# Cutting HBM into blocks of 8, 60 and 60 rows per partition in a streaming x + gamma*y kernel, with the small block loaded first and stored in the middle

## The chip, the core and the metric

The kernel runs on one core of a Trainium2 chip. Time is device time in microseconds (us), as the median over several executions. Spans and packet durations come from one profiled execution of each kernel.

## The reference

```python
# x, y: [1024, 16, 512] bfloat16, gamma: [512] bfloat16
def reference(x, y, gamma):
    return x + gamma * y
```

Flattened, x and y are 16384 rows of 512 elements, 1 KB each. Each of the 128 SBUF partitions gets 128 rows. Reading x and y and writing the result moves 3 x 16.78 = 50.33 MB, and there is little arithmetic.

## The kernel before

Partition p holds rows 128p to 128p + 127, so the same row of neighbouring partitions lies 128 KiB apart in HBM. The loads go out on SyncE's queue in the order of the list `SP`, the stores on ScalarE's in the order of `ACT`. VectorE works in place on y, in four pieces; `m` is the multiply by gamma, `a` the addition of x.

```python
PIECES = [53, 11, 53, 11]
SP = [('y', 0, 4), ('y', 4, 64), ('x', 0, 64, 0), ('y', 64, 128), ('x', 64, 117, 0), ('x', 117, 128, 64)]
ACT = [('g',), ('s', 0, 64), ('s', 64, 128)]
RELEASE = ('x', 64, 117, 0)
DVE = [('m', 0), ('m', 1), ('a', 0), ('a', 1), ('m', 2), ('m', 3), ('a', 2), ('a', 3)]
...
xv = xf.rearrange("(p n) d -> p n d", p=P)      # the same for y and out
...
# a load of x waits until the adds that read its buffer slots are done;
# the first store waits until RELEASE has landed, and every store for its adds
```

An entry `('x', 64, 117, 0)` loads rows 64 to 117 of every partition into slot 0 and up of x's buffer. That buffer has fewer slots than there are rows, so this load has to wait for the first add. The first two loads are issued ahead of everything else. The first store is released by the landing of `RELEASE`, so that stores do not share the DMA engines with the loads that VectorE needs.

Of the kernel before, what the change touches and what calls it, by code (L numbers as in the profile page):

```python
# [3 lines left out]


PIECES = [53, 11, 53, 11]



SP = [('y', 0, 4), ('y', 4, 64), ('x', 0, 64, 0), ('y', 64, 128), ('x', 64, 117, 0), ('x', 117, 128, 64)]  # L10
ACT = [('g',), ('s', 0, 64), ('s', 64, 128)]

EARLY = (2, 0)


RELEASE = ('x', 64, 117, 0)

DVE = [('m', 0), ('m', 1), ('a', 0), ('a', 1), ('m', 2), ('m', 3), ('a', 2), ('a', 3)]
MULT, ADD = mybir.AluOpType.mult, mybir.AluOpType.add


def _take(sem, n, eng):


    return eng.wait_ge(sem, n).then_inc(sem, -n)  # L25


def kernel(
# [10 lines left out]
    P = nc.NUM_PARTITIONS  # L39
# [3 lines left out]
    xf = x.flatten_outer_dims()  # L43
    yf = y.flatten_outer_dims()
    of = out.flatten_outer_dims()
    N, D = xf.shape
    rows = N // P
    n = len(PIECES)
    assert sum(PIECES) == rows
    starts = [sum(PIECES[:c]) for c in range(n + 1)]  # L50
    dt = xf.dtype
    xv = xf.rearrange("(p n) d -> p n d", p=P)
    yv = yf.rearrange("(p n) d -> p n d", p=P)
    ov = of.rearrange("(p n) d -> p n d", p=P)

    gamma_row = nc.alloc_sbuf_tensor("gamma_row", [1, D], dt).ap()
    ones_row = nc.alloc_sbuf_tensor("ones_row", [1, P], dt).ap()
# [1 line left out]
    y_sb = nc.alloc_sbuf_tensor("y_sb", [P, rows, D], dt).ap()  # L59
    x_loads = [w for w in SP + ACT if w[0] == "x"]  # L60
    y_loads = [w for w in SP + ACT if w[0] == "y"]
    stores = [w for w in SP + ACT if w[0] == "s"]
    for loads in (x_loads, y_loads, stores):
# [7 lines left out]
    s_load = {w: sem("s_" + "_".join(map(str, w[:2]))) for w in x_loads + y_loads}  # L71
    s_add, s_go, s_rel, s_end, s_out = sem("s_add"), sem("s_go"), sem("s_rel"), sem("s_end"), sem("s_out")
    added = [a for kind, *a in DVE if kind == "a"]
    order = {a[0]: k for k, a in enumerate(added)}

    def meets(a, b, c, d):
        return a < d and c < b

    def pieces_of(a, b):
        return [c for c in range(n) if meets(starts[c], starts[c + 1], a, b)]  # L80

    def x_at(row):
        return next(w[3] + row - w[1] for w in x_loads if w[1] <= row < w[2])

    def frees(w):

        c = set()
        for v in x_loads[: x_loads.index(w)]:
            lo, hi = max(v[3], w[3]), min(v[3] + v[2] - v[1], w[3] + w[2] - w[1])
            if lo < hi:  # L90
                c |= set(pieces_of(v[1] + lo - v[3], v[1] + hi - v[3]))
        return sorted(c)
# [3 lines left out]
    def ring(eng, what, n_early):  # L96

        known, went = 0, False
        for k, w in enumerate(what):
            kind = w[0]  # L100
            need = frees(w) if kind == "x" else pieces_of(w[1], w[2]) + list(w[3:]) if kind == "s" else []
            need = max((order[c] + 1 for c in need), default=0)
            if kind == "s" and not went:
                _take(s_go, 1, eng)
                went = True
            if need > known:
                eng.wait_ge(s_add, need)
                known = need
            if kind == "g":
                i = eng.dma_start(out=gamma_row, in_=gamma.unsqueeze(0)).then_inc(s_gamma, 16)  # L110
            elif kind == "x":
                to = x_sb[:, w[3] : w[3] + w[2] - w[1], :]
                i = eng.dma_start(out=to, in_=xv[:, w[1] : w[2], :]).then_inc(s_load[w], 16)
            elif kind == "y":
                r = slice(w[1], w[2])
                i = eng.dma_start(out=y_sb[:, r, :], in_=yv[:, r, :]).then_inc(s_load[w], 16)
            else:
                r = slice(w[1], w[2])
                i = eng.dma_start(out=ov[:, r, :], in_=y_sb[:, r, :]).then_inc(s_out, 16)
            if k < n_early:  # L120
                early.append(i.ins)

    ring(nc.sync, SP, EARLY[0])
    ring(nc.scalar, ACT, EARLY[1])


# [7 lines left out]

    _take(s_load[RELEASE], 16, nc.tensor)
    nc.tensor.sem_inc(s_go, 1)
# [4 lines left out]
    def need(loads, c):  # L141
        for w in loads:
            if w not in landed and meets(starts[c], starts[c + 1], w[1], w[2]):
                if w == RELEASE:
                    _take(s_rel, 1, nc.vector)
                else:
                    _take(s_load[w], 16, nc.vector)
                landed.add(w)

    for kind, *args in DVE:  # L150
        c = args[0]
        yt = y_sb[:, starts[c] : starts[c + 1], :]
        if kind == "m":
            need(y_loads, c)
            g = gamma_sb[:, None, :].to_broadcast([P, PIECES[c], D])
            nc.vector.tensor_tensor(out=yt, in0=yt, in1=g, op=MULT).then_inc(s_dve, 1)  # L156
            open_mults += 1
        else:
# [4 lines left out]
            at = x_at(starts[c])  # L163
            xt = x_sb[:, at : at + PIECES[c], :]
            nc.vector.tensor_tensor(out=yt, in0=xt, in1=yt, op=ADD).then_inc(s_add, 1)  # L165
# [44 lines left out]
```

## Time and profile before

| | before |
|---|---|
| median time | 120.06 us |
| profiled span | 118.7 us |
| VectorE busy | 70.0 us (59%) |
| packets in the 16 DMA engines | 98.6% of the span |
| bytes, mean rate | 50.33 MB, 424 GB/s |
| 64 KB packet | 2418 ns, loads and stores alike |

Some figures here and below come from the trace's record of each DMA packet (start, duration, size, queue), summed over the packets and divided by 16 engines. "Idle" is the time in which fewer than 16 packets are in flight, weighted by how many are missing. "Extra" is what packets take above 0.03677 ns per byte + 8.4 ns.

### The profile page before, as it was taken

How to read it: one execution, taken by the hardware profiler on the slowest of the kernel's cores; microseconds unless marked ns; L12 is line 12 of the kernel's file. 1: busy time of each engine (PE TensorE's matmuls, PEld its weight loads, DVE VectorE, ACT ScalarE, POOL GpSimd, SP SyncE). 2: the span in 40 equal slices, each digit the busy share in tenths (PEclk: the TensorE clock that was granted, in tenths of full speed). 3: DMA queues.
4: the chain of work that ended last, by engine and by line, in shares of the span. 5: the costliest groups of instructions: out<-in, count | busy, mean ns of one | idle time of the engine just before them, and what ended most of it. 6: DMA issues, size and time to landing. Idle time of an engine off the chain costs nothing. (4 is left out here: it accounts for less than half of the span.)

```text
span 118.7 us, 80 instructions
## 1 busy us (share of the span) xinstructions
PE 0.6 (0%) x1; PEld 0.1 (0%) x1; DVE 70.0 (59%) x10; POOL 0.2 (0%) x4
## 2 busy tenths in 40 slices
PE   0001000000000000000000000000000000000000
PEld 0000000000000000000000000000000000000000
DVE  0002000599999299999759999999999910000000
POOL 0000000000000000000000000000000000000000
DMA  8977977998899888998896969498899889988891
GB/s 268 571 332 331 663 331 331 596 464 353 353 486 574 353 353 353 640 420 353 353 585 293 585 293 585 205 634 353 353 596 464 353 353 420 640 353 353 353 663 44
DMA packets 1154, 50.33 MB, mean 424 GB/s; under 512 B 129, under 2 KB 130, under 8 KB 258
## 3 DMA queue, kind: packets, MB, share of 16 engines
q1 hardware_dynamic: 864, 33.55, 66.0%
q10 hardware_dynamic: 290, 16.78, 32.6%
HBM read 33.56 MB, written 16.78 MB: 424 GB/s over the span
## 5 line engine op out<-in xcount | busy, mean ns | idle before, releaser
L156 DVE TENSOR_TENSOR y_sb<-y_sb,gamma_sb 128x27136 bf16<-128x27136 bf16 (+1 forms) x4 | 34.6, 8688 | 12.3 <-DVEq L25 12.3
L165 DVE TENSOR_TENSOR y_sb<-x_sb,y_sb 128x27136 bf16<-128x27136 bf16 (+1 forms) x4 | 34.6, 8689 | 2.3 <-DVEq L25 2.2
L132 DVE CAST gamma_sb<-gamma_ps 128x512 bf16<-128x512 f32 x1 | 0.7, 692 | 8.8 <-DVEq L25 8.8
L127 DVE MEMSET ones_row<- 1x128 bf16 x1 | 0.2, 165 | 2.0 <-PEq L41 2.0
L130 PE MATMUL gamma_ps<-gamma_row,ones_row 1*128 1x512 bf16 x1 | 0.6, 577 | 10.2 <-PEq L25 10.2
L130 PEld LDWEIGHTS gamma_ps<-gamma_row,ones_row 1*128 1x128 bf16 x1 | 0.1, 99 | 10.2 <-issue 10.2
L194 POOL MEMSET const-bfloat16-1.0<- 128x1 bf16 x1 | 0.1, 101 | 0.0
L194 POOL MEMSET const-uint8-127<- 128x1 uint8 x1 | 0.1, 101 | 0.0
L194 POOL MEMSET const-float32-0.0<- 128x1 f32 x1 | 0.1, 98 | 0.2 <-issue 0.2
L194 POOL MEMSET const-float32-1.0<- 128x1 f32 x1 | 0.1, 98 | 0.0
## 6 DMA issues: line engine op xcount, KB each, us to landing
y_sb<-in_y_dram SPq DMA_DIRECT2D x1, 7680.0 KB, 21.4
x_sb<-in_x_dram SPq DMA_DIRECT2D x1, 6784.0 KB, 20.8
x_sb<-in_x_dram SPq DMA_DIRECT2D x1, 1408.0 KB, 23.8
y_sb<-in_y_dram SPq DMA_DIRECT2D x1, 512.0 KB, 3.8
out_dram<-y_sb ACTq DMA_DIRECT2D x2, 22.8
x_sb<-in_x_dram SPq DMA_DIRECT2D x1, 39.3
gamma_row<-in_gamma_dram ACTq DMA_DIRECT2D x1, 1.0 KB
y_sb<-in_y_dram SPq DMA_DIRECT2D x1, 58.3
```

The costliest lines, as they stand in the source:

```text
L127: nc.vector.memset(ones_row, 1.0).then_inc(s_ones, 1)
L130: nc.tensor.matmul(gamma_ps, ones_row, gamma_row, start=True, stop=True).then_inc(s_ps, 1)
L132: nc.vector.tensor_copy(out=gamma_sb, in_=gamma_ps).then_inc(s_dve, 1)
L156: nc.vector.tensor_tensor(out=yt, in0=yt, in1=g, op=MULT).then_inc(s_dve, 1)
L165: nc.vector.tensor_tensor(out=yt, in0=xt, in1=yt, op=ADD).then_inc(s_add, 1)
L194: nc = _bacc.Bacc("TRN2", target_bir_lowering=False, num_devices=1)
```

## The change

The intent is to make each block that is loaded or stored contiguous in HBM, to begin with a small contiguous block of y, and to put that block's store between the two large stores.

```diff
+BLOCKS = [8, 60, 60]
-PIECES = [53, 11, 53, 11]
+PIECES = [49, 19, 49, 11]
-SP = [('y', 0, 4), ('y', 4, 64), ('x', 0, 64, 0), ('y', 64, 128), ('x', 64, 117, 0), ('x', 117, 128, 64)]
-ACT = [('g',), ('s', 0, 64), ('s', 64, 128)]
+SP = [("y", 0, 8), ("y", 8, 68), ("x", 0, 8, 0), ("x", 8, 68, 8),
+      ("y", 68, 128), ("x", 68, 117, 0), ("x", 117, 128, 49)]
+ACT = [("g",), ("s", 8, 68), ("s", 0, 8), ("s", 68, 128)]
-RELEASE = ('x', 64, 117, 0)
+RELEASE = ("x", 68, 117, 0)
...
-    xv = xf.rearrange("(p n) d -> p n d", p=P)
+    def rows_of(t, a, b):
+        c = max(c for c in range(len(BLOCKS)) if edges[c] <= a)
+        block = t[P * edges[c] : P * edges[c + 1]].rearrange("(p n) d -> p n d", p=P)
+        return block[:, a - edges[c] : b - edges[c], :]
```

(The lists are broken over fewer lines than in the file, and an assertion and the three uses of `rows_of` are left out.) Partition p now holds 8 rows of the first block, 60 of the second and 60 of the third; the pitch between partitions is 8 KiB in the first and 60 KiB in the two others.

More of the change, by code (lines that the diff above doesn't have):

```diff
@@ L3 @@
 from concourse import mybir
-PIECES = [53, 11, 53, 11]
-SP = [('y', 0, 4), ('y', 4, 64), ('x', 0, 64, 0), ('y', 64, 128), ('x', 64, 117, 0), ('x', 117, 128, 64)]
-ACT = [('g',), ('s', 0, 64), ('s', 64, 128)]
+BLOCKS = [8, 60, 60]
+PIECES = [49, 19, 49, 11]
+SP = [
+    ("y", 0, 8),
+    ("y", 8, 68),
+    ("x", 0, 8, 0),
+    ("x", 8, 68, 8),
+    ("y", 68, 128),
+    ("x", 68, 117, 0),
+    ("x", 117, 128, 49),
+]
+ACT = [("g",), ("s", 8, 68), ("s", 0, 8), ("s", 68, 128)]
 EARLY = (2, 0)
-RELEASE = ('x', 64, 117, 0)
-DVE = [('m', 0), ('m', 1), ('a', 0), ('a', 1), ('m', 2), ('m', 3), ('a', 2), ('a', 3)]
+RELEASE = ("x", 68, 117, 0)
+DVE = [("m", 0), ("m", 1), ("a", 0), ("a", 1), ("m", 2), ("m", 3), ("a", 2), ("a", 3)]
 MULT, ADD = mybir.AluOpType.mult, mybir.AluOpType.add
@@ L51 @@
     dt = xf.dtype
-    xv = xf.rearrange("(p n) d -> p n d", p=P)
-    yv = yf.rearrange("(p n) d -> p n d", p=P)
-    ov = of.rearrange("(p n) d -> p n d", p=P)
+    edges = [sum(BLOCKS[:c]) for c in range(len(BLOCKS) + 1)]
+    assert edges[-1] == rows
+    def rows_of(t, a, b):
+        c = max(c for c in range(len(BLOCKS)) if edges[c] <= a)
+        assert b <= edges[c + 1]
+        block = t[P * edges[c] : P * edges[c + 1]].rearrange("(p n) d -> p n d", p=P)
+        return block[:, a - edges[c] : b - edges[c], :]
     gamma_row = nc.alloc_sbuf_tensor("gamma_row", [1, D], dt).ap()
@@ L112, in ring @@
                 to = x_sb[:, w[3] : w[3] + w[2] - w[1], :]
-                i = eng.dma_start(out=to, in_=xv[:, w[1] : w[2], :]).then_inc(s_load[w], 16)
+                i = eng.dma_start(out=to, in_=rows_of(xf, w[1], w[2])).then_inc(s_load[w], 16)
             elif kind == "y":
                 r = slice(w[1], w[2])
-                i = eng.dma_start(out=y_sb[:, r, :], in_=yv[:, r, :]).then_inc(s_load[w], 16)
+                i = eng.dma_start(out=y_sb[:, r, :], in_=rows_of(yf, w[1], w[2])).then_inc(s_load[w], 16)
             else:
                 r = slice(w[1], w[2])
-                i = eng.dma_start(out=ov[:, r, :], in_=y_sb[:, r, :]).then_inc(s_out, 16)
+                i = eng.dma_start(out=rows_of(of, w[1], w[2]), in_=y_sb[:, r, :]).then_inc(s_out, 16)
             if k < n_early:
```

## The prediction

> **What bounds the kernel now.** The kernel computes x + gamma*y on bf16, so it must read x and y and write the result: 3 x 16.78 MB = 50.33 MB. I first read the page's totals.
>
> ```profile
> span 118.7 us, 80 instructions
> ...
> PE 0.6 (0%) x1; PEld 0.1 (0%) x1; DVE 70.0 (59%) x10; POOL 0.2 (0%) x4
> ...
> DMA packets 1154, 50.33 MB, mean 424 GB/s; under 512 B 129, under 2 KB 130, under 8 KB 258
> ...
> q1 hardware_dynamic: 864, 33.55, 66.0%
> q10 hardware_dynamic: 290, 16.78, 32.6%
> ```
>
> No engine is near the span: VectorE, the only one with work, has 70.0 us of 118.7. The two DMA queues (q1 the loads from SyncE, q10 gamma and the stores from ScalarE) have packets in the 16 DMA engines for 66.0 + 32.6 = 98.6% of the span, 117.0 us. Only 1.7 us of DMA time is unused. The next question is where that is, so I cut the span at the places where one transfer follows another.
>
> ```profile
> 0.00:3.40 3.40, 0.00 (x0) 0.00 (x0) 0.17 (x1) 0.20 (x4) 1.00 1.24 443
> 3.40:21.00 17.60, 0.58 (x1) 0.10 (x1) 0.69 (x1) 0.00 (x0) 1.00 0.91 395
> 21.00:59.70 38.70, 0.00 (x0) 0.00 (x0) 34.59 (x4) 0.00 (x0) 1.00 1.00 435
> 59.70:79.00 19.30, 0.00 (x0) 0.00 (x0) 18.16 (x3) 0.00 (x0) 1.00 0.99 427
> 79.00:117.50 38.50, 0.00 (x0) 0.00 (x0) 16.43 (x2) 0.00 (x0) 1.00 1.01 437
> 117.50:118.70 1.20, 0.00 (x0) 0.00 (x0) 0.00 (x0) 0.00 (x0) 1.00 0.01 0
> ```
>
> The columns are the stretch, its length, busy time of the compute engines, the clock, the share of the 16 DMA engines, and GB/s. A packet is counted where it starts, so a stretch can show a little over 1.00 and its neighbour under it; the long ones show what matters: 435 GB/s for the two loads of 64 rows (21.0 to 59.7) and 437 for the stores (79.0 to 117.5), with nothing missing in between.
>
> The trace's packet records say the same more sharply. A 64 KB packet takes 2418 ns, a 60 KB one 2267, a 53 KB one 2004, an 11 KB one 422, a 4 KB one 159, with hardly any scatter, in loads and stores alike. A straight line through 159 and 2418 is 0.03677 ns per byte (27.2 GB/s an engine, 435 for 16) plus 8.4 ns per packet. First packet 1.0 us after the first issue, last packet end 118.34 us; between them all 16 engines have a packet nearly always: summed over the engines, idle time is 1.58 us per engine, of which 1.2 is the start and 0.38 the ragged end (0.36 us after the last packet is counted neither in it nor in the packets). One more loss: the 128 4-KB packets of the first load take 0.64 us per engine more than the line gives, because the first packet of each engine needs some 0.2 to 1.2 us. So the floor for this volume, 50.33 MB at 0.03677 ns per byte over 16 engines, is 115.7 us, and the kernel is 3.0 us above it in the profile.
>
> Last, do waits leave slack? VectorE and the issues in order of time, and the SyncE queue's waits:
>
> ```profile
> 21.99 17.29 DVE L156 TENSOR_TENSOR y_sb<-y_sb,gamma_sb 128x27136 bf16<-128x27136 bf16 x2 [10.33 <-DVEq L25]
> 41.46 17.29 DVE L165 TENSOR_TENSOR y_sb<-x_sb,y_sb 128x27136 bf16<-128x27136 bf16 x2 [2.17 <-DVEq L25]
> 55.78 0.81 SPq L113 DMA_DIRECT2D x_sb<-in_x_dram  x2
> 60.69 17.29 DVE L156 TENSOR_TENSOR y_sb<-y_sb,gamma_sb 128x27136 bf16<-128x27136 bf16 x2 [1.94 <-DVEq L25]
> 76.95 18.85 ACTq L119 DMA_DIRECT2D out_dram<-y_sb  x2
> 78.13 17.30 DVE L165 TENSOR_TENSOR y_sb<-x_sb,y_sb 128x27136 bf16<-128x27136 bf16 x2
> ```
> ```profile
> SPq L113 <- DVE y_sb L165: 53.0, 1, 53.0
> ```
>
> The 53.0 us wait is for buffer reuse: x of rows 64 to 117 goes where x of rows 0 to 53 lay, and is issued only after the first add. It goes out at 55.78; the loads ahead of it last until 59.7 to 60.2, so it costs nothing, with 3.9 us to spare. The first store goes out at 76.95, when x of rows 64 to 117 has landed; the last 11 rows of x, 3.4 us of DMA time, keep the engines busy until its first packet at 79.06. The second store goes out near 95.5, and the first lasts until about 98.5. So three hand-overs, each covered.
>
> **What the Trainium skill says.** "DMA: Bandwidth & Descriptors", section Bandwidth, gives a ceiling of 435 GB/s (16 ports of 32 bytes at 850 MHz); the 435 and 437 measured here agree, so the middle of this kernel is at the limit. The same page, section Latency and other measured facts, reports that HBM row pitches at large powers of two slow copies (207 GB/s at a pitch of 512 KiB, less at 2 MiB and above). The kernel before has a pitch of 128 KiB between partitions, which the change replaces by 8 and 60 KiB; but as packets at 128 KiB pitch already run at 435, this trace shows no loss that contiguous blocks could win back. The same page under "Queues, rings and completion order" says an engine takes turns between queues packet by packet; the gamma row, issued at 1.9 us and moved at 7.5 behind two or three 60 KB packets, agrees with queueing behind packets already taken up. "HBM Reference", Specifications, has a lone core at about 425 GB/s bounded by its DMA engines; the mean here is 424.
>
> **The change part by part.** Bytes stay the same. The order of built instructions shows VectorE with the same four multiplies and four adds in the same order, at 49, 19, 49 and 11 rows in place of 53, 11, 53 and 11.
>
> 1. *More packets.* Loads go from 6 to 7 and stores from 2 to 3 (gamma apart). Each is 128 packets, 8 an engine, so 16 more packets an engine: 16 x 8.4 ns = 0.13 us. Two more completion packets at 9 ns and the small gaps around them: 0.03. Sum +0.16 us.
>
> 2. *The first load.* It is 8 KB per partition rather than 4, and 1 MB in one piece. The first-packet latency, most of the 0.64 us, stays: first bytes still come after 1.0 us. Neighbouring partitions are now 8 KB rather than 128 KB apart, which might shorten the scatter of the first packets. I guess -0.1 us, between +0.1 and -0.4. This is a choice, not a reading.
>
> 3. *VectorE.* From 14291 ns for 27136 elements and 3085 for 5632, an operation costs 150 ns + 0.521 ns per element: 49 rows 13.22 us, 19 rows 5.22, 11 rows 3.09. A row of all partitions is 64 KB packets' 2420/64 per KB times 8 an engine, 0.3025 us. The first half is now 68 rows, 4 more: y lands 1.2 us later, so multiplies run about 23.2 to 41.6. x to row 68 is 8 rows' time later than before: adds start 43.9, the first is done at 57.1, the second at 62.3. The second half's multiplies run 62.4 to 78.7, its adds 78.7 to 95.0. None of this is on the path unless a hand-over fails.
>
> 4. *Hand-overs.* x of 68 to 117 is issued at 57.2; y of 68 to 128 drains at 60.2 + 1.2 = 61.4: 4.2 us to spare. x of 117 to 128 now waits too, since its slots 49 to 60 held rows the second add reads: issued at 62.4, wanted at about 76: harmless. The first 245 rows loaded are the same amount, so x of row 117 lands at the same 76.2 plus 0.1, the store is issued at about 77.0, and the same 11 rows cover it. Rows 8 to 68 then 0 to 8 are stored, 68 rows in all, until about 99.9; the last store is issued at 95.1, 4.8 us ahead instead of about 3.4. All stay hidden: 0 us.
>
> 5. *The end.* Last packets are 60 KB, 2267 ns instead of 2418. That does not shorten the sum; it may trim the ragged 0.38 us by a few hundredths. I take 0.
>
> Sum: +0.16 - 0.1 = +0.06, on 120.06 us: 120.1 us. (The 1.36 us between time and profile span I leave as it is.)
>
> **The rivals.** *Contiguous blocks make HBM faster.* It would need packets below 2418 ns per 64 KB; the constant durations for loads and stores, and the flat 435, speak against it. Only the start, 0.64 us in all, could gain: at best 119.5. *A hand-over opens.* The tightest is loads to stores: issued 76.95, first packet 79.06, just as the last load packets end, so part of that 2.1 us may be real latency. Should the start of a store of 60 rows take longer, or the queue lose its cover, each engine could idle up to 0.5 us: 120.6. The same amount of cover (11 rows) speaks against. *The small store in the middle costs more than packets.* 8 KB writes may not stream as the large ones do; 8 packets of 310 ns an engine is only 2.5 us of work, so even 20% is 0.5 us: again 120.6. The 11 KB loads at 422 ns against a line's 422.6 say that small packets stream, though no store here is small. *The wait on the second add stalls the ring.* It would need VectorE 13 us late; excluded.
>
> **Range and chances.** The floor of 115.7 leaves 3.0 us, nearly all start and end latency, so gaining 2% (2.4 us) would need almost all of it; losing 2% needs a hand-over with a gap of over 2 us, where I found 4 us of slack or unchanged cover. Hence 97% within 2%, 1% faster, 2% slower. Plus or minus half a microsecond covers the start's scatter and a small gap: 119.6 to 120.5.
>
> **What would show it.** In the changed profile: DMA packets 1154 + 2 x 144 = 1442; 60 KB packets at 2267 ns for loads and stores; the two queues together near 98.6% of a span near 118.8; no idle stretch of the engines at 60, 76 to 80 and 99 us; VectorE's starts as in step 3. I am wrong if packet durations change with the layout, if the first load's extra 0.64 us shrinks or grows by more than 0.3, or if a gap opens at the loads-to-stores turn.

## The result

The changed kernel takes 120.14 us (119.98 to 120.27, 5 runs) against 120.06 us (119.98 to 120.15, 5 runs). Ratios here are the mean time of one kernel's runs over that of the other's of the same rounds, so they are not quite the ratio of the medians. This one is 1.0001, with a 95% interval of 0.9989 to 1.0013: the same time. Measured again on one chip with other kernels, it was 120.01 us, ratio 0.9995 (0.9981 to 1.0009).

From the page of the changed kernel, the lines of span, packets and queues:

```profile
span 118.8 us, 83 instructions
...
PE 0.6 (0%) x1; PEld 0.1 (0%) x1; DVE 69.9 (59%) x10; POOL 0.2 (0%) x4
...
DMA packets 1442, 50.33 MB, mean 424 GB/s; under 512 B 161, under 2 KB 162, under 8 KB 162
...
q1 hardware_dynamic: 1008, 33.55, 65.7%
q10 hardware_dynamic: 434, 16.78, 32.6%
```

There are 1442 packets instead of 1154, with the same bytes and the same mean rate, and the engines hold packets for 65.7 + 32.6 = 98.3% of the span. VectorE, the issues and the waits of SyncE's queue in the changed kernel, in order of time (start, duration, instruction, idle before it), answer to those shown of before:

```profile
23.14 18.36 DVE L171 TENSOR_TENSOR y_sb<-y_sb,gamma_sb 128x25088 bf16<-128x25088 bf16 x2 [12.36 <-DVEq L34]
43.89 18.36 DVE L180 TENSOR_TENSOR y_sb<-x_sb,y_sb 128x25088 bf16<-128x25088 bf16 x2 [2.39 <-DVEq L34]
57.14 5.46 SPq L128 DMA_DIRECT2D x_sb<-in_x_dram  x2
62.17 16.22 DVE L171 TENSOR_TENSOR y_sb<-y_sb,gamma_sb 128x25088 bf16<-128x25088 bf16 x2
77.06 18.07 ACTq L134 DMA_DIRECT2D out_dram<-y_sb  x3
78.53 16.23 DVE L180 TENSOR_TENSOR y_sb<-x_sb,y_sb 128x25088 bf16<-128x25088 bf16 x2
```
```profile
SPq L128 <- DVE y_sb L180: 58.7, 2, 53.9
```

The wait on the adds now comes twice, as both last loads of x reuse slots. None of it reaches the DMA engines. Cut at the ends of the changed kernel's own transfers, the stretches are:

```profile
22.50:61.00 38.50, 0.00 (x0) 0.00 (x0) 35.47 (x4) 0.00 (x0) 1.00 1.00 434
61.00:79.00 18.00, 0.00 (x0) 0.00 (x0) 17.85 (x4) 0.00 (x0) 1.00 1.01 433
79.00:100.00 21.00, 0.00 (x0) 0.00 (x0) 15.76 (x2) 0.00 (x0) 1.00 1.05 454
100.00:117.50 17.50, 0.00 (x0) 0.00 (x0) 0.00 (x0) 0.00 (x0) 1.00 0.96 418
```

The last two columns are the share of the DMA engines and GB/s. The last two lines belong together, because a packet is counted where it starts: 21.0 x 454 + 17.5 x 418, over 38.5 us, is 438 GB/s. The packet records show no idle time between the start and the ragged end, in either kernel.

### The profile page after: what moved, and what is told of

Its sections match the earlier page's. It is cut to its first block, busy times and chain, and to the rows that moved or that the text cites. A ratio compares the mean times of both kernels' runs of the same rounds, so it can differ in the third digit from the quotient of the medians.

```text
span 118.8 us, 83 instructions
## 1 busy us (share of the span) xinstructions
PE 0.6 (0%) x1; PEld 0.1 (0%) x1; DVE 69.9 (59%) x10; POOL 0.2 (0%) x4
## 2 busy tenths in 40 slices
DMA packets 1442, 50.33 MB, mean 424 GB/s; under 512 B 161, under 2 KB 162, under 8 KB 162
## 3 DMA queue, kind: packets, MB, share of 16 engines
q1 hardware_dynamic: 1008, 33.55, 65.7%
q10 hardware_dynamic: 434, 16.78, 32.6%
## 5 line engine op out<-in xcount | busy, mean ns | idle before, releaser
L171 DVE TENSOR_TENSOR y_sb<-y_sb,gamma_sb 128x25088 bf16<-128x25088 bf16 (+2 forms) x4 | 34.6, 8687 | 12.4 <-DVEq L34 12.4
L180 DVE TENSOR_TENSOR y_sb<-x_sb,y_sb 128x25088 bf16<-128x25088 bf16 (+2 forms) x4 | 34.6, 8688 | 2.5 <-DVEq L34 2.4
## 6 DMA issues: line engine op xcount, KB each, us to landing
out_dram<-y_sb ACTq DMA_DIRECT2D x1, 1024.0 KB, 23.2
```

The costliest lines, as they stand in the source:

```text
L171: nc.vector.tensor_tensor(out=yt, in0=yt, in1=g, op=MULT).then_inc(s_dve, 1)
L180: nc.vector.tensor_tensor(out=yt, in0=xt, in1=yt, op=ADD).then_inc(s_add, 1)
```

## The experiments

Twelve runs were made, all with correct results, in three groups of four. The kernels of a group ran on one chip beside the kernel before, whose medians were 120.05, 120.05 and 120.07 us; five rounds were asked for, which gave 4 to 6 timed runs of each kernel.

**Layout alone.** The schedule of before, in two contiguous blocks of 64 rows (pitch 64 KiB).

```diff
 (against the changed kernel)
-BLOCKS = [8, 60, 60]
+BLOCKS = [64, 64]
 PIECES, SP, ACT and RELEASE as in the kernel before
```

> Layout alone: the schedule of before (same transfers, same row counts), but the tensors cut into two contiguous blocks of 64 rows per partition, so that the pitch between partitions is 64 KiB instead of 128 KiB. My theory (the DMA engines are at a per-engine rate that the layout doesn't touch): 64 KB packets stay at 2418 ns, time 120.06 +- 0.15 us. Rival (contiguous blocks make HBM faster, and the change only came out even because its extra packets ate the gain): 119.8 or less, with the start's extra packet time below 0.4 us instead of 0.64.

Measured: 120.73 us, ratio 1.0051 (1.0038 to 1.0064). Both expectations fell: this layout is slower, by 0.6 us. The order of time shows where VectorE and the stores fall behind:

```profile
22.52 17.29 DVE L170 TENSOR_TENSOR y_sb<-y_sb,gamma_sb 128x27136 bf16<-128x27136 bf16 x2 [10.24 <-DVEq L33]
41.98 17.29 DVE L179 TENSOR_TENSOR y_sb<-x_sb,y_sb 128x27136 bf16<-128x27136 bf16 x2 [2.16 <-DVEq L33]
...
61.22 17.29 DVE L170 TENSOR_TENSOR y_sb<-y_sb,gamma_sb 128x27136 bf16<-128x27136 bf16 x2 [1.95 <-DVEq L33]
77.60 18.73 ACTq L133 DMA_DIRECT2D out_dram<-y_sb  x2
```

Against before, 0.53 us are lost by the first multiply (22.52 against 21.99), nothing more up to 61 us, and another 0.12 by the first store (77.60 against 76.95). The packet records agree: of the 64 packets of 60 KB that start before 12 us, 18 take over 2290 ns, up to 2992; of the 128 packets of 11 KB, 15 take over 450 ns, up to 674. In the kernel before these counts are 1 and 2. Of the 128 packets of 53 KB, 24 take over 20 ns too long, against 7. The 64 KB packets, loads and stores, stay at 2418. So this layout slowed some reads, at the start and where packets shrink, and not the long streams.

**Order alone.** The changed kernel at the old pitch.

```diff
-        block = t[P * edges[c] : P * edges[c + 1]].rearrange("(p n) d -> p n d", p=P)
-        return block[:, a - edges[c] : b - edges[c], :]
+        return t.rearrange("(p n) d -> p n d", p=P)[:, a:b, :]
```

> Order alone: transfers, stores and VectorE pieces of the changed kernel, but at the old pitch of 128 KiB between partitions. My theory: 120.06 + 0.16 (16 more packets an engine) = 120.1 to 120.3 us, same packet durations as the changed kernel, and the first load's packets cost about the same as in the changed kernel, because their size and not their pitch sets that. Rival (layout gains about what the packets lose): 120.4 or more.

Measured: 119.94 us, ratio 0.9992 (0.9979 to 1.0004), just under the range of my theory. The other half of that theory fell too: at the old pitch the 8 KB load packets carry 0.60 us of extra, in the changed kernel 0.37, so their cost does depend on the pitch (step 2 below tells why that gained nothing). With 120.14 for the changed kernel this looked like a layout that costs 0.2 us, and so I ran both on one chip.

> The changed kernel once more, on one chip with the next three, because the run with its order at the old pitch came out at 119.94 us, 0.2 under its recorded 120.14. If its layout costs nothing: 119.95 to 120.1, the same as the next run within 0.1. If the layout costs about 0.2: 120.1 to 120.25 and the next run 119.9 to 120.0, with a gap between them that the five rounds separate.

> The changed order at the old pitch of 128 KiB again, beside the changed kernel itself. Layout free: within 0.1 us of the run before it. Layout costs: 0.15 to 0.25 us less than it, with the start (idle before the engines are full, plus the first packets' extra) some 0.15 us shorter, as in the first profile of this kernel (1.74 against 1.88).

Measured: 120.01 us, ratio 0.9995 (0.9981 to 1.0009), for the changed kernel and 120.11 us, ratio 1.0001 (0.9989 to 1.0013), for its order at the old pitch. The sign has turned over. The 0.2 us was the difference of two runs' scatter; at 8/60/60 the layout's effect on the time is too small to see here.

**A third layout under the changed order.** `BLOCKS = [68, 60]`, one line changed, to see whether any shorter pitch costs what 64 KiB did.

> A third layout under the changed order: two blocks of 68 and 60 rows instead of 8, 60 and 60, so pitches of 68 and 60 KiB. If the 0.6 us that two blocks of 64 rows lost belongs to a pitch of exactly 64 KiB, this stays at 119.95 to 120.2, with 11 KB packets at 422 to 434 ns. If any shorter pitch costs that much: 120.4 to 120.7, with 11 KB packets up to 600 ns and more, as there.

Measured: 120.02 us, ratio 0.9993 (0.9980 to 1.0005). One 11 KB packet of 128 takes over 450 ns. The loss goes with the blocks of 64 rows, and not with contiguous blocks as such. Why they lose is open: 64-row blocks were run under the old order only, the other layouts under the new one, and no run tells whether it is the pitch of 64 KiB or how it meets that order's packet sizes.

**More packets.** In the changed kernel every transfer of 49 or 60 rows is cut in four.

```diff
-    ("y", 8, 68),
+    *[("y", 8 + 15 * i, 23 + 15 * i) for i in range(4)],
 (the same for x of 8 to 68, y of 68 to 128, x of 68 to 117 and the two large stores;
  RELEASE is the last part of x of 68 to 117)
```

> The packet cost enlarged: in the changed kernel each transfer of 49 or 60 rows (four loads, two stores) is cut in four, bytes and order unchanged. 18 more DMAs, 144 more data packets an engine, 18 more completion packets. My theory (8.4 ns a packet, about 15 ns a completion with its gap, and nothing hides it because the DMA engines are the bound): 144 x 8.4 + 18 x 15 = 1.5 us more than the changed kernel, 121.6 us (121.2 to 121.9). Rival (the 8.4 ns are an artefact of how packets are recorded and overlap): 120.1 to 120.4.

Measured: 121.18 us (121.03 to 121.28), ratio 1.0096 (1.0081 to 1.0111), just below the range. The page's line of packets for this kernel:

```profile
DMA packets 4034, 50.33 MB, mean 420 GB/s; under 512 B 449, under 2 KB 450, under 8 KB 450
```

The added packets are 4034 - 1442 = 2592, or 162 an engine (144 of data, 18 completions). Against the kernel before the time is up by 0.0096 x 120.05 = 1.15 us, and the changed kernel's own ratio is 1 within the noise, so a data packet with its share of completions costs 1.15/144 = 8.0 ns, give or take 1.3 from the interval; I had put some 10 ns on it. It is a real cost. A part of the difference is at the end: with 15 KB packets the ragged end is 0.15 us, as against 0.15 and 0.34 in the two profiles of the changed kernel.

The rival was also half right: packets overlap. Summed and divided by 16, the durations grow by 1.8 us (116.9 to 118.7). But what exceeds 16 packets in flight, which such a sum counts twice, grows from 0.29 to 0.87 us; in a steady stream the next packet starts 3 to 4 ns before the last one ends. So the 8.4 ns of the durations are not the cost in time, which is read from start to start (mean start of one group of 16 packets to that of the next, medians): the 15 KB stores come every 569.5 ns, the 15 KB loads every 572.9. Less 564.8 for their bytes, a store packet costs 4.7 ns and a load packet 8.1. With 96 more loads, 48 more stores and 18 completions of 9 ns, that is an estimate of some 1.2 us, in line with the 1.15 measured.

**The cover taken away.** The stores are released by the last load.

```diff
-RELEASE = ("x", 68, 117, 0)
+RELEASE = ("x", 117, 128, 49)
```

> The cover of the turn from loads to stores taken away: in the changed kernel the stores are released by the landing of the last load (rows 117 to 128 of x) instead of the one before it. My theory: the last load packet ends near 79.7, the store is issued some 0.65 us later (77.06 against 76.39 in the changed kernel), and its first packet needs 1.0 us (as at the start) to 2.1 us (as seen behind the cover): the engines idle 1.7 to 2.9 us, time 121.8 to 123.0 us. Rival (the DMA engines weren't short of work at the turn anyway, or the small store absorbs it): 120.1 to 120.6.

Measured: 121.92 us (121.89 to 121.94), ratio 1.0155 (1.0141 to 1.0169). Stretches around the turn and the stores' issue, in this kernel:

```profile
77.00:79.50 2.50, 0.00 (x0) 0.00 (x0) 2.35 (x2) 0.00 (x0) 1.00 0.81 342
79.50:81.10 1.60, 0.00 (x0) 0.00 (x0) 1.60 (x1) 0.00 (x0) 1.00 0.00 0
81.10:97.00 15.90, 0.00 (x0) 0.00 (x0) 13.62 (x2) 0.00 (x0) 1.00 1.00 433
```
```profile
80.30 14.79 ACTq L134 DMA_DIRECT2D out_dram<-y_sb  x3
```

No packet starts between 79.5 and 81.1 us. The packet records give 1.95 us of idle per engine, about the 1.86 us lost (0.0155 x 120.05). The first 16 store packets after the gap take 2316 to 2332 ns instead of 2267, which is little. The first store packet starts at 81.17, 0.9 us after the issue at 80.30. So most of the 2.1 us that lay between issue and first packet in the kernel before was waiting behind the last load, and not latency. That hand-over had about 1.2 us to spare, in both kernels: 2.1 - 0.9 before, and 79.21 - 77.06 - 0.9 = 1.2 in the changed one, where the first store packet starts at 79.21.

**Slack at the reuse of x's buffer.** A useless multiply on VectorE ahead of the first add, of n x 512 elements into free PSUM.

```diff
+            if c == 0:
+                g = gamma_sb[:, None, :].to_broadcast([P, 3, D])     # 7 in the second kernel
+                nc.vector.tensor_tensor(out=spare_ps, in0=g, in1=g, op=MULT)
```

> Slack at the reuse of x's buffer: one useless multiply of 3 x 512 elements into PSUM, placed in the changed kernel after x has landed and before the first add. By the 0.69 us of the 512-element cast out of PSUM it should take 1.6 to 2.1 us. The load of x from row 68 is then issued near 59.0, its first packet can come at 60.0 to 61.1, the engines run out at 61.0 to 61.4: hidden, 120.1 us (up to 120.3). If VectorE were on the path: +1.6 to 2.1 us.

> The same with 7 x 512 elements, 3.7 to 4.8 us. The load is then issued at 60.9 to 61.9, its first packet can come 1.0 to 2.1 us later, after the engines have run out at 61.0 to 61.4: idle 0.7 to 2.5 us at that place, time 120.8 to 122.6 us. If the slack is larger than I read (the 1.0 us between issue and first packet does not count, because the queue still has work), 120.1 to 120.4.

Measured: 120.38 us, ratio 1.0031 (1.0017 to 1.0045), with n = 3, and 122.38 us, ratio 1.0192 (1.0175 to 1.0209), with n = 7. The kernel with n = 7, in order of time, and then its DMA share around the hand-over:

```profile
43.76 3.90 DVE L182 TENSOR_TENSOR spare_ps<-gamma_sb 128x3584 f32<-128x3584 bf16 x1 [2.38 <-DVEq L34]
47.57 18.35 DVE L185 TENSOR_TENSOR y_sb<-x_sb,y_sb 128x25088 bf16<-128x25088 bf16 x2
60.81 5.46 SPq L130 DMA_DIRECT2D x_sb<-in_x_dram  x2
```
```profile
59.10:61.70 2.60, 0.00 (x0) 0.00 (x0) 2.60 (x2) 0.00 (x0) 1.00 0.00 0
61.70:79.00 17.30, 0.00 (x0) 0.00 (x0) 17.30 (x3) 0.00 (x0) 1.00 0.99 411
```

The load goes out at 60.81, and its first packet starts 1.0 us later, after the engines have begun to run out near 60.8. (A zero in the first stretch does not mean idle for all of it: packets that began before 59.1 still run in it. The records give 1.03 us of idle.) Yet the kernel loses 2.3 us. The profiled execution is the fastest of the four (122.08); its last packet ends 1.94 us later than in the changed kernel's profile, and this can be accounted for. Idle time is 1.03. The first packets after the gap are slow, 1907 to 2956 ns for the first 16, instead of 1853 for 49 KB: packets outside the start carry 0.74 us of extra, against 0.07. The ragged end is 0.70 instead of 0.34, and the start 0.13 shorter. So this gap in the loads cost more than its idle time. The gap before the stores, in the run without cover, did not: 1.95 us of idle time, 1.86 lost. Why loads restart slowly and stores do not was not tested. With the delay of 1.77 us (n = 3) the load is issued at 58.82 and the records show no idle time at the hand-over, as expected; but the time is 0.3 us longer, a little over the 120.3 that I allowed. The profiled execution was the fastest of the five (120.19), and shows nothing that explains the others; this 0.3 us stays open.

**The first load.** Two edits of the kernel before: 8 rows in place of 4, and no small first load at all.

```diff
-SP = [('y', 0, 4), ('y', 4, 64), ...
+SP = [('y', 0, 8), ('y', 8, 64), ...      # the first kernel
+SP = [('y', 0, 64), ...                   # the second
```

> The kernel before with its first load of 8 instead of 4 rows (the second of 56 instead of 60) and nothing else changed; as many packets as before. If the first load's size gains what the order gained at the old pitch: 119.8 to 119.9 us, and idle time plus extra packet time at the start 0.1 to 0.2 us under the 1.84 of before. If it does nothing: 120.0 to 120.1.

> The kernel before without a small first load: y of rows 0 to 64 in one transfer. 8 packets an engine fewer, so by the packet cost 120.05 - 0.07 = 120.0 us if a small first load is of no use; the start's idle time and first-packet extra then stay at 1.8. If small first packets are what gets all 16 engines going, the start grows by some tenths: 120.2 to 120.6.

Measured: 119.98 us, ratio 0.9999 (0.9984 to 1.0013), and 119.97 us, ratio 0.9998 (0.9983 to 1.0013). Idle time and extra at the start are 1.85 and 1.86 us, as before (1.85). The first load's size is of no use and no harm.

**The small store first.** `ACT = [("g",), ("s", 0, 8), ("s", 8, 68), ("s", 68, 128)]` in the changed kernel.

> The small store moved to the front of the stores in the changed kernel, so that its 8 KB packets follow the turn from loads to stores. My theory (8 KB stores stream at 309 ns a packet wherever they stand): 120.1 us +- 0.15, no idle at 79. Rival (the small store needs a large one around it): idle at the turn, 120.3 or more.

Measured: 119.92 us (119.92 to 119.96, 4 runs), ratio 0.9989 (0.9976 to 1.0003), 0.03 us under the expected range, with no idle time at the turn. No effect of the small store's place can be seen. It is the lowest median of all, but the interval holds 1, so this is no version that beats both.

## Why the prediction was right, point by point

The time, 120.14 us, lies at the 120.1 that was predicted and within 119.6 to 120.5, for the main reason given: the DMA engines are full from the first packet to the last, and the change moves the same bytes at the same rate. The run without cover shows it from the other side: the engines idled 1.95 us, and the kernel lost about that. The packets are as forecast too: those of 60 KB take 2267 ns, loads and stores alike. That the sum hits the median to 0.04 us is luck, as its two terms (+0.16 and -0.1) are too small to be seen here and the second was a guess that failed.

1. *More packets, +0.16 us.* The packet count of 1442 is exact, and the cost per packet is real, but its size was read from durations, which overlap. With 8 load packets at 8.1 ns and 8 store packets at 4.7, 16 packets are an estimate of 0.10 us instead of 0.13. (The overlap also explains why the prediction finds 1.7 us unused by the page, and 1.58 + 0.36 = 1.94 us by the records: in the kernel before, more than 16 packets are in flight for 0.25 us.) In the time of the changed kernel itself it cannot be seen: two groups gave ratios of 1.0001 and 0.9995, each plus or minus 0.12 to 0.14%, or 0.15 us.

2. *The first load, -0.1 us, a guess.* It did not come out as guessed, in an instructive way. The extra of the packets that start before 6 us fell from 0.65 to 0.38 us (the 0.64 of the prediction counts the 4 KB packets alone), but the idle time at the start rose from 1.20 to 1.51, since ten of the 16 engines start their first packet only at 1.65 to 1.81 us, and all by 1.26 in the kernel before. In all seven profiles at 8/60/60 the idle time is 1.31 to 1.51 and the extra 0.35 to 0.52; in the six at pitches of 128 or 68 KiB they are 1.14 to 1.23 and 0.56 to 0.67. The sum is 1.75 to 1.90 in all thirteen. Time has moved from one column to the other, and the step is worth 0. The prediction's own sign of being wrong, a first load whose extra changes by more than 0.3, was only just not met (0.64 to 0.37).

3. *VectorE.* Starts predicted at 23.2, 43.9, 62.4 and 78.7 us came at 23.14, 43.89, 62.17 and 78.53.

4. *Hand-overs, 0 us.* Right: no idle time in the middle. The two issues, predicted at 57.2 and 95.1, came at 57.14 and 94.79. What I took as the tightest, loads to stores, is the tightest, with 1.2 us to spare. At x's buffer the 4.2 us I counted must be cut by the 1.0 us between issue and first packet: 1.77 us of delay leave no idle time, 3.90 us do. One slip: the second store of the kernel before was "about 3.4" us ahead by the prediction, but its own 98.5 and 95.5 give 3.0 (2.9 in the records).

5. *The end, 0 us.* The ragged end was 0.34 and 0.15 us in two profiles of the changed kernel, 0.38 in before's. That is the scatter of one execution and no effect of the change.

Of the rivals, "contiguous blocks make HBM faster" is not borne out: the changed kernel and its order at the old pitch differ by 0.2 us one way and 0.1 the other, and the layout of 64-row blocks is slower by 0.6 us. The prediction's argument, that the full rate at 128 KiB leaves nothing for a new layout to win, held; that a layout could lose time it did not argue, though packet durations that change with the layout stand among its signs of being wrong. The blocks of 64 rows lose 0.6 us; that 8/60/60 loses nothing is measured and not explained.

## What to carry to other kernels

When the DMA queues' shares add up to the span, count bytes and packets first, then check only whether each hand-over stays covered: issue time + about 1 us against the time when the engines run out. A gap costs at least about its idle time; the one in the loads cost about twice that, the one before the stores no more. Read the cost of a packet from start to start, since durations overlap. Do not name a cause for 0.2 us until both kernels have run on one chip side by side; here the sign turned over.

## What the Trainium skill lacked or had wrong

- "DMA: Bandwidth & Descriptors", Latency and other measured facts, names row pitches of 512 KiB and above, at large powers of two, as slow. Here a pitch of 128 KiB ran at full rate, and 64 KiB, in two blocks under the same schedule, lost 0.6 us (120.73 against 120.05), in reads at the start and in 11 KB packets (up to 674 ns instead of 422); stores kept their 2418 ns. 68, 60 and 8 KiB, under the changed order, lost nothing that could be seen. That the pitch alone is the cause is not shown.
- The same page, Queues, rings and completion order, has nothing on how deep a queue's packets are taken up in advance: when the first store was issued, 2.1 us before its first packet, each engine had about five 11 KB load packets still to start, and about three 0.9 us later, the time from issue to first packet with empty queues; nearly all of them went ahead of the stores.
- The same section does not say what a restart costs: after 1.03 us of idle time, first load packets of 49 KB took up to 2956 ns instead of 1853, and the kernel lost 2.3 us; after 1.95 us, first store packets of 60 KB took up to 2332 ns instead of 2267, and it lost 1.86.
- The same page, Why small descriptors are slow, has about 3 cycles of fixed cost per packet (at the page's 850 MHz an estimate of 3.5 ns) and 32 bytes of metadata per operation, with no difference between loads and stores. Here a 15 KB packet costs 4.7 ns of time beyond its bytes as a store and 8.1 as a load; the 8.4 ns in the durations overlap with the next packet by 3 to 4.
